# Attention and gated mixing on one core: the table that orders the program is replaced (2,239 pieces reordered, 219 on another engine)

## The chip, the cores and the metric

The kernel runs on one core of a Trainium2 chip. The core has five engines that run side by side, each through its own queue in order: TensorE (PE in the rows, its weight loads PEld), VectorE (DVE), ScalarE (ACT), GpSimd (POOL) and SyncE (SP), which here issues nearly all DMAs. Engines wait for each other by semaphores. The metric is the device time of one execution in microseconds; lower is better.

## The reference

```python
def _attn_ref(q, k, v):                      # q, k, v: 8 x 8 heads x 576 x 64
    k_p = k.reshape(B, H, Sp, pool, D).mean(axis=3)      # pool = 8, Sp = 72
    v_p = v.reshape(B, H, Sp, pool, D).mean(axis=3)
    scores = scale * np.matmul(q, k_p.transpose(0, 1, 3, 2))
    attn = np.exp(scores - max); attn = attn / (sum + 1e-09)
    return np.matmul(attn, v_p)

def _moe_ref(x, w_theta, w_tok_r, w_tok_i, w_ch):        # x: 8 x 576 x 512
    theta = x @ w_theta
    zr, zi = x * np.cos(theta), x * np.sin(theta)
    y = np.einsum('ts,bsd->btd', w_tok_r, zr) + np.einsum('ts,bsd->btd', w_tok_i, zi)
    u = x + y
    return u + np.maximum(u @ w_ch, 0.0)
```

The four weights arrive as 8-byte floats and are turned into 4-byte ones on the core.

## The kernel before, in words

The kernel is a set of generators, one for each small job. Each `yield` ends one piece: an instruction or a few that belong together. The string `SCHEDULE` names the pieces in the order in which they are written into the program; a word is the name of a generator, and a last letter v, g or a says whether VectorE, GpSimd or ScalarE does this piece where there is a choice. Since every engine goes through its queue in order, the table sets the order on all engines, and the order of SP's loads as well. No other code decides the order.

The jobs, with the batch as first number: `k`, `v` load keys and values, `K`, `V` pool them by 8; for batch 0 TensorE does the pooling (tiles `kpp`, `vpp`, L608, L610). The second half of `K` turns the pooled keys (`pk` L619 and `pkr` L629, both on TensorE) and copies them to the one tile `kpT`, which all score matmuls read. `Q` loads and turns queries (`pq` L670, tile `qT`). `S` makes scores (`s`, L762), their maximum, exponential and normalisation (`en`). `E` turns the attention of a batch by 16 small DMAs (L913), `X` multiplies with the values (`pv` L964). `T` (L991 to L1062) makes the angles (`pt`), sines and cosines and the product with x, which it writes to the tile `z`: for the last tokens of batch 0 the line of ScalarE is L995, of VectorE L997 and L1051, then the sine L1053 and the product L1055. `Z` splits a slice of `z` in a high and a low part (`zh`, `zl`), `M` mixes tokens with it (`py`, L1091, 27 matmuls a piece group), `F` is the last product with `w_ch` and the output (`pf`, L1119, L1135). `h`, `w`, `W` and `c` convert and turn the weights; `w_theta` arrives by way of `WTh_st` and becomes `ths`. `D` is a warm-up: 12 matmuls of the identity with itself, whose result nothing reads:

```python
    def warm_up():
        p = bank([P, 512], "av", "warm")
        for _ in range(12):
            nc.tensor.matmul(p[:, 0:P], ident, ident, start=True, stop=True)
        yield
```

The first `py` needs all of `z` of batch 0, so all nine token tiles of both weights and the whole of attention for batch 0 stand ahead of it. From there to the end each batch's `M` and `F` are woven with the next batches' `S`, `X` and `T`.

Of the kernel before, what the change touches and what calls it, by code (L numbers as in the profile page):

```python
# [1255 lines left out]
```

## Time and profile before

| | |
|---|---|
| median of 3 runs | 596.73 us (596.09 to 597.28) |
| the profiled execution | 598.02 us, span 596.2 us |
| PE busy | 580.1 us, 97% of the span |
| DVE, POOL, ACT busy | 456.2, 362.3, 319.0 us |
| DMA | 56.88 MB, mean 95 GB/s |

The profiled execution took 598.02 us on its own clock, 1.8 us more than the span between its first and last instruction, and 1.3 us more than the median of the runs.

### The profile page before, as it was taken

Reading aid. Unit: us, or ns where it says so; the run is one execution under the profiler, and the core shown is the slowest. Engines: PE = TensorE matmul, PEld = TensorE weight load, DVE = VectorE, ACT = ScalarE, POOL = GpSimd, SP = SyncE. Lnnn points to the kernel's source line nnn. Section 1 sums busy time; section 2 is a strip of 40 time slices with the busy share of each in tenths; the row PEclk is TensorE's granted clock in tenths of the full one; section 3 lists DMA queues with packets and bytes.
Section 4 is the critical chain, followed back from the end, with each engine's and each line's share of the span. In section 5 each row is a group of like instructions: output and inputs, shape, how many; then the busy total and the mean of one; then the engine's idle time right before and its main releaser. Section 6 shows DMA issues by size and latency. Waiting matters only on the chain.

```text
span 596.2 us, 11701 instructions
## 1 busy us (share of the span) xinstructions
PE 580.1 (97%) x4072; PEld 540.2 (91%) x4072; DVE 456.2 (77%) x857; ACT 319.0 (54%) x684; POOL 362.3 (61%) x517
## 2 busy tenths in 40 slices
PE   8799989999999999999999999999999999999996
PEld 7577879988999989999999999999999999999996
DVE  5989988888878897578969888887867688555434
ACT  3989987766457664186336663355434464432100
POOL 5562646567867885786878773754757665342620
PEclk9999979999999999999999999999999999999999
DMA  7995221576354273552555253562522310201214
GB/s 229 263 328 120 73 71 46 121 128 120 96 95 98 64 147 67 129 103 78 97 117 111 65 125 92 105 124 45 90 62 61 73 29 15 57 1 30 41 20 82
DMA packets 174203, 56.88 MB, mean 95 GB/s; under 512 B 148416, under 2 KB 162752, under 8 KB 174144
## 3 DMA queue, kind: packets, MB, share of 16 engines
q1 hardware_dynamic: 169280, 55.55, 42.1%
q10 hardware_dynamic: 4864, 0.59, 0.6%
q8 instruction: 32, 0.52, 0.4%
q14 instruction: 27, 0.22, 0.1%
HBM read 37.81 MB, written 9.44 MB: 79 GB/s over the span
## 4 chain that ended last, share of the span: by engine, by line
PE 81%; DVE 9%; ACT 5%; SPq 2%; issue 2%; DMA 1%; POOL 0%; DVEq 0%; POOLq 0%; ACTq 0%
PE py L1091 34%; PE pt L991 14%; PE pf L1119 14%; PE pv L964 6%; PE s L762 5%; PE px L1034 2%; SPq L913 1%; PE warm L310 1%; ACT e_eps L805 1%; PE kpp L608 1%; PE s L754 1%; PE vpp L608 1%; DVE mx L796 1%; DVE g L997 1%; SPq L642 1%
## 5 line engine op out<-in xcount | busy, mean ns | idle before, releaser
L1091 PE MATMUL py<-WTh,zh 128*128 128x256 f32 (+1 forms) x576 | 88.1, 298 | 0.7 <-DVE z L1060 0.6
L1091 PE MATMUL py<-WTl,zh 128*128 128x256 f32 (+1 forms) x576 | 87.3, 295 | 0.0
L1091 PE MATMUL py<-WTh,zl 128*128 128x256 f32 (+1 forms) x576 | 86.4, 296 | 0.0
L1091 PEld LDWEIGHTS py<-WTh,zh 128*128 128x128 f32 x576 | 80.4, 190 | 1.3 <-ACT zh L213 0.9
L1091 PEld LDWEIGHTS py<-WTl,zh 128*128 128x128 f32 x576 | 80.5, 189 | 0.2
L1091 PEld LDWEIGHTS py<-WTh,zl 128*128 128x128 f32 x576 | 78.6, 188 | 0.6
L198 POOL TENSOR_TENSOR zl<-z,zh 128x384 fp32r<-128x384 f32 (+1 forms) x80 | 63.8, 828 | 15.3 <-ACT zh L213 12.7
L198 POOL TENSOR_TENSOR en<-e_eps,ri 128x256 f32<-128x256 f32 (+3 forms) x66 | 38.3, 601 | 37.0 <-DVE ri L821 22.2
L995 ACT ACTIVATE g<-pt,c_magic 128x512 f32<-128x512 f32 x35 | 24.0, 686 | 54.7 <-PE pt L991 52.3
L1119 PE MATMUL pf<-uh,chh 128*128 128x256 f32 (+1 forms) x256 | 44.8, 298 | 0.5 <-DVE xb L1124 0.5
L1119 PE MATMUL pf<-uh,chl 128*128 128x256 f32 (+1 forms) x256 | 44.7, 296 | 0.0
L1119 PE MATMUL pf<-ul,chh 128*128 128x256 f32 (+1 forms) x256 | 44.0, 294 | 0.0
L991 PE MATMUL pt<-th,xh 128*128 128x512 f32 x148 | 41.8, 404 | 0.7 <-DVE xh L215 0.4
L991 PE MATMUL pt<-th,xl 128*128 128x512 f32 x148 | 40.5, 395 | 0.1
L991 PE MATMUL pt<-tl,xh 128*128 128x512 f32 x148 | 40.3, 394 | 0.0
L762 PE MATMUL s<-kpT,qT 128*128 128x144 f32 x256 | 38.4, 294 | 1.7 <-DVE ri L821 1.1
L1119 PEld LDWEIGHTS pf<-uh,chh 128*128 128x128 f32 x256 | 38.0, 188 | 2.3 <-DVE xb L1124 1.0
L1097 DVE TENSOR_TENSOR xb<-py,xb 128x320 f32<-128x320 f32 x32 | 15.2, 479 | 31.8 <-PE py L1091 31.8
L997 DVE SCALAR_TENSOR_TENSOR g<-g,pt 128x512 f32<-128x512 f32 x35 | 23.8, 681 | 18.9 <-ACT g L995 18.6
L762 PEld LDWEIGHTS s<-kpT,qT 128*128 128x128 f32 x256 | 34.9, 194 | 3.2 <-issue 1.4
L1119 PEld LDWEIGHTS pf<-uh,chl 128*128 128x128 f32 x256 | 37.4, 188 | 0.2
L1119 PEld LDWEIGHTS pf<-ul,chh 128*128 128x128 f32 x256 | 37.3, 188 | 0.0
(275 smaller groups left out, 1407.5 us busy)
## 6 DMA issues: line engine op xcount, KB each, us to landing
kpst<-in_k_dram SPq DMA_DIRECT2D x15, 512.0 KB, 4.3
vpst<-in_v_dram SPq DMA_DIRECT2D x28, 256.0 KB, 4.1
qsst<-in_q_dram SPq DMA_DIRECT2D x96, 72.0 KB, 3.2
eraw<-G SPq DMA_DIRECT2D x144, 40.0 KB, 1.9
out_dram<-R SPq DMA_DIRECT2D x112, 40.0 KB, 1.7
out_dram<-R SPq DMA_DIRECT2D x112, 32.0 KB, 1.7
eraw<-G SPq DMA_DIRECT2D x48, 60.0 KB, 2.0
WTh_st<-in_moe_w_theta_dram SPq DMA_DIRECT2D x4, 512.0 KB, 9.1
```

The costliest lines, as they stand in the source:

```text
L198: nc.gpsimd.tensor_tensor(out[:, r], a[:, r], b[:, r], op)
L310: nc.tensor.matmul(p[:, 0:P], ident, ident, start=True, stop=True)
L608: nc.tensor.matmul(main[:, 2 * j : 2 * j + 2, :], ident, st[:, :, D * r : D * r + D], **steps[r])
L762: nc.tensor.matmul(scs[c // 2][:n, 2 * SP * (c % 2) : 2 * SP * (c % 2 + 1)], qT[:, c, t0 : t0 + n], kpT[:, c, :], start=True, stop=True,)
L964: nc.tensor.matmul(pv[:, :gn], l, r, start=i == 0, stop=i == len(terms) - 1)
L991: nc.tensor.matmul(pt, l[:, c, :], r[:, c, :], start=i == 0, stop=i == 11)
L995: nc.scalar.activation(g, pt, AF.Identity, bias=c_magic)
L997: nc.vector.scalar_tensor_tensor(g, g, MAGIC, pt, ALU.subtract, ALU.subtract)
L1034: nc.tensor.transpose(px[:, P * c : P * c + P], x[:, c], ident)
L1091: nc.tensor.matmul(py[:, :n], l[:, kk, :], r[:, kw, t], start=i == 0, stop=i == 3 * NK - 1)
L1097: nc.vector.tensor_tensor(u, py[:, :n], u, ALU.add)
L1119: nc.tensor.matmul(pv[:, :n], l[:, kk, o], uhl[r][:, kk, t], start=i == 0, stop=i == 11)
```

## The change

Only `SCHEDULE` changes. The same 2,239 words stand in it in another order, on average 10.6 places away from where they stood, and 219 words end in another letter: 56 from VectorE to GpSimd and 44 back, 37 from VectorE to ScalarE and 33 back, 26 from GpSimd to ScalarE and 23 back. The instructions, tiles and buffers are the same.

```diff
 SCHEDULE = """
-k0.0 D K0.0 h0 h0 h0v h0v h0 h0 h0g k0.1 K0.0a K0.1 Q0.0 Q0.0 Q0.0v K0.1a K0 K0a h0 h0v h0 h2 h2 h2g h2v h2 k0.2 h1
-Q0.1 K0.2 K0.2a K0 K0a S0.0 S0.0 h1 h1a Q0.1 Q0.1v h1a h1 h1 h1g Q0.4 Q0.4 S0.0 S0.0 h2 Q0.4v S0.1 S0.1 S0.1 S0.1 k1.2
...
+k0.0 K0.0 K0.0a h0 h0 k0.1 K0.1 K0.1a K0 K0a h0g h0v h0 h0 h0v Q0.0 Q0.0 h0 k0.2 K0.2 K0.2v K0 K0v h0v Q0.0a S0.0 h2
+S0.0 h2 h2g h2a h2 h1 h1 Q0.1 Q0.1 D Q0.3 h0 Q0.1v S0.1 k1.2 h1v h1a S0.0 S0.0 h1 h1 S0.1 S0.1 S0.1 Q0.2 Q0.2 Q0.2v h2
...
```

Three places show what this does to the queues.

The first is TensorE's queue at the start of the program. Before:

```order
1 L310 MATMUL warm<-ident 128x128 x12
2 L608 MATMUL kpp_132<-kpst_0_117,ident 128x128 x8
3 L608 MATMUL kpp_132<-z,ident 128x128 x8
4 L670 MATMUL pq_0_166<-ident,qsst_0_164 128x128 x4
5 L619 MATMUL pk_173<-ident,kp_152 64x128 x4
6 L428 MATMUL ths_181<-WTh_st,ident 128x512
7 L429 MATMUL ths_181<-WTl_st,identr 128x512
8 L610 MATMUL kpp_132<-kprst_192,ident 64x64 x8
9 L629 MATMUL pkr_205<-ident,kpr_153 64x64
10 L762 MATMUL s_0_208<-kpT,qT_163 128x144 x4
11 L670 MATMUL pq_1_217<-ident,qsst_0_164 128x128 x4
12 L670 MATMUL pq_4_230<-ident,qst_228 128x64 x4
```

And in the changed kernel:

```order
1 L608 MATMUL kpp_119<-kpst_0_117,ident 128x128 x8
2 L608 MATMUL kpp_119<-z,ident 128x128 x8
3 L619 MATMUL pk_145<-ident,kp_128 64x128 x4
4 L670 MATMUL pq_0_162<-ident,qsst_0_160 128x128 x4
5 L428 MATMUL ths_167<-WTh_st,ident 128x512
6 L429 MATMUL ths_167<-WTl_st,identr 128x512
7 L610 MATMUL kpp_119<-kprst_170,ident 64x64 x8
8 L629 MATMUL pkr_181<-ident,kpr_129 64x64
9 L762 MATMUL s_0_186<-kpT,qT_159 128x144 x4
10 L670 MATMUL pq_1_202<-ident,qsst_0_160 128x128 x4
11 L310 MATMUL warm<-ident 128x128 x12
12 L762 MATMUL s_1_0_223<-kpT,qT_159 128x144 x2
```

The warm-up has moved from the first place to behind the first scores and the second block of queries (`pq_1`), and ahead of the second scores (`s_1`); the queries `pq_4` went further back.

The second place is SP's queue of loads at the start; `kprst` with 64x512 is the last part of a batch's keys, `z` stands in for buffers of queries and of values, `wraw` is a block of token weights. Before:

```order
8 L663 DMA qsst_0_164<-in_q_dram 128x8x64
9 L663 DMA qst_228<-in_q_dram 64x8x64
10 L564 DMA kprst_268<-in_k_dram 64x512
11 L663 DMA z<-in_q_dram 128x8x64 x2
12 L406 DMA WTh_st<-in_moe_w_theta_dram 128x1024
13 L457 DMA wraw_0_359<-in_moe_w_tok_r_dram 128x1152
14 L552 DMA kpst_1_390<-in_k_dram 128x2x512
15 L555 DMA z<-in_v_dram 64x2x512 x4
```

And in the changed kernel:

```order
7 L663 DMA qsst_0_160<-in_q_dram 128x8x64
8 L663 DMA z<-in_q_dram 128x8x64
9 L564 DMA kprst_229<-in_k_dram 64x512
10 L663 DMA z<-in_q_dram 128x8x64
11 L406 DMA WTh_st<-in_moe_w_theta_dram 128x1024
12 L663 DMA qst_315<-in_q_dram 64x8x64
13 L457 DMA wraw_0_372<-in_moe_w_tok_r_dram 128x1152
14 L555 DMA z<-in_v_dram 64x2x512 x4
15 L566 DMA vprst_418<-in_v_dram 64x1x512
16 L552 DMA kpst_1_444<-in_k_dram 128x2x512
```

One block of queries now stands ahead of `kprst` of batch 1, and the four loads of batch 0's values stand ahead of `kpst_1`, the 512 KB of batch 1's keys.

The third place is ScalarE's queue just before the first `py`, where the keys of batch 1 go into `kpT` and the last part of `z` is made. Before:

```order
96 L995 ACTIVATE g_4_923<-pt_4_889,c_magic 128x512
97 L213 CAST WTh<-wt_8_911 128x128
98 L1042 ACTIVATE xaspare<-xaspare,c_cos 128x512
99 L1053 ACTIVATE sn_4_935<-g_4_923,c_half 128x512
100 L213 COPY kpT<-pk_948 64x4x72
101 L213 COPY kpT<-pk_948 64x3x72
102 L213 COPY kpT<-pk_948 64x8
103 L213 COPY kpT<-pkr_956 64x64
104 L213 CAST zh_0_959<-z 128x2x9x64
```

And in the changed kernel:

```order
100 L995 ACTIVATE g_4_931<-pt_4_916,c_magic 128x512
101 L213 CAST WTh<-wt_8_945 128x128
102 L213 COPY kpT<-pk_954 64x4x72
103 L213 COPY kpT<-pk_954 64x3x72
104 L213 COPY kpT<-pk_954 64x8
105 L1042 ACTIVATE xaspare<-xaspare,c_cos 128x512
106 L1053 ACTIVATE sn_4_943<-g_4_931,c_half 128x512
107 L213 CAST zh_0_968<-z 128x2x9x64
108 L213 CAST zh_1_971<-z 128x2x9x64
```

The three copies from `pk` now stand ahead of the cosine (L1042) and the sine (L1053); the copy from `pkr` has left ScalarE and stands in VectorE's queue, behind the products L1047 and L1055 that end `z`. On TensorE the queries `pq_4` of batch 1, which stood between the scores `s` and the first `py`, now stand some 20 rows earlier.

## Rows read from the trace of the kernel before

**Rows 1.** The page: span, busy time of each engine, its share, instructions

```profile
span 596.2 us, 11701 instructions
PE 580.1 (97%) x4072; PEld 540.2 (91%) x4072; DVE 456.2 (77%) x857; ACT 319.0 (54%) x684; POOL 362.3 (61%) x517
```

**Rows 2.** Windows: length; PE, PEld, DVE, ACT, POOL busy; PE clock, DMA, GB/s

```profile
0.00:20.00 20.00, 16.83 (x116) 14.71 (x116) 13.57 (x27) 10.56 (x35) 9.21 (x18) 1.00 0.82 229
20.00:40.00 20.00, 17.37 (x121) 12.55 (x120) 16.95 (x35) 17.89 (x83) 14.12 (x22) 1.00 1.06 317
40.00:60.00 20.00, 19.84 (x117) 14.21 (x115) 19.55 (x39) 18.41 (x32) 5.39 (x8) 1.00 0.60 155
60.00:80.00 20.00, 17.10 (x106) 14.52 (x105) 17.75 (x33) 18.31 (x35) 14.04 (x18) 0.94 0.25 79
```

**Rows 3.** Waits of PE from 100 us to its end: us in total, times, longest

```profile
PE py L1091 <- DVE z L1060: 0.6, 1, 0.6
...
PE pt L991 <- DVE g L997: 0.2, 1, 0.2
```

**Rows 4.** Timeline of PE, 0 to 34 us: start, us, what, [idle before]

```profile
1.36 5.12 PE L310 MATMUL warm<-ident 128*128 128x128 f32 x24 [1.36 <-POOL ident masks.py:199]
6.54 2.05 PE L608 MATMUL kpp<-kpst,ident 128*128 128x128 f32 x16
8.95 2.05 PE L608 MATMUL kpp<-z,ident 128*128 128x128 f32 x16 [0.35 <-ACT kp L213]
...
14.51 1.25 PE L762 MATMUL s<-kpT,qT 128*128 128x144 f32 x8
...
17.20 1.25 PE L762 MATMUL s<-kpT,qT 128*128 128x144 f32 x8 [0.62 <-DVE qT L215]
...
21.11 1.22 PE L762 MATMUL s<-kpT,qT 128*128 128x144 f32 x8 [1.08 <-DVE ri L821]
...
28.39 3.83 PE L608 MATMUL vpp<-z,ident 128*128 128x128 f32 x32 [0.84 <-ACT wsrc_a L377]
```

**Rows 5.** The waits of PE's sequencer at L608 for the keys' loads

```profile
L608 PEldq EVENT_SEMAPHORE  x2: 51/51/51, 4.4 to 8.2; - x2
```

**Rows 6.** Timeline of SP's queue, 5 to 21 us

```profile
5.63 2.66 SPq L663 DMA_DIRECT2D qst<-in_q_dram  x1
14.07 0.49 SPq L564 DMA_DIRECT2D kprst<-in_k_dram  x1
...
18.26 2.81 SPq L555 DMA_DIRECT2D z<-in_v_dram  x4
```

**Rows 7.** Timeline of PE, ACT and DVE around the first py

```profile
72.93 1.08 PE L991 MATMUL pt<-th,xl 128*128 128x512 f32 x4
...
77.14 0.78 ACT L213 COPY kpT<-pk 64x288 f32<-64x288 f32 x3
77.60 0.67 DVE L1055 TENSOR_TENSOR z<-px,sn 128x512 f32<-128x512 f32 x1
...
77.97 0.31 PE L629 MATMUL pkr<-ident,kpr 64*64 64x64 f32 x1 [2.46 <-ACT kpT L213]
...
78.22 2.29 PE L762 MATMUL s<-kpT,qT 128*128 128x144 f32 x8
...
78.55 1.15 ACT L213 CAST zh<-z 128x1152 fp32r<-128x1152 f32 x1
...
80.44 0.69 PE L670 MATMUL pq<-ident,qst 64*128 64x64 f32 x4
...
81.05 2.29 PE L1091 MATMUL py<-WTh,zh 128*128 128x256 f32 x9
```

**Rows 8.** Windows, same columns as rows 2

```profile
78.00:81.00 3.00, 3.00 (x13) 2.54 (x13) 1.33 (x3) 1.93 (x3) 1.55 (x1) 0.50 0.03 8
81.00:84.00 3.00, 3.00 (x16) 2.95 (x15) 2.93 (x6) 2.64 (x6) 0.00 (x0) 0.50 0.00 0
...
85.00:86.00 1.00, 1.00 (x9) 1.00 (x8) 1.00 (x3) 1.00 (x8) 0.00 (x0) 1.00 0.53 74
```

More of the change, by code (lines that the diff above doesn't have):

```diff
@@ new lines @@
+T1.0g T1.0 M0.1.1a M0.3.1 S1.4v Q2.0 Q2.0 S1.4 S1.4a S1.4 S1.4 S1.4a k2.0 K2.0g T1.0 M0.3.0g M0.1.0a T1.0 T1.0 k2.2
+S1.4 X1.2.1 X1.2.1v K2 v2.0 F0.3.0 K2a X1.2.2 M0.0.0v X1.2.2a M0.3.0g F0.3.0 K2.2g K2 X1.2.0 T1.0 T1.0 M0.1.0g F0.3.0
+T1.0 X1.2.0v M0.0.1g V2.0v X1.2.3 X1.2.3a T1.2a T1.2g X1.2.3g M0.1.1g M0.3.1 T1.0a T1.0 T1.0 T1.0 Q2.1 Q2.1 T1.1a
+T1.1g M0.3.1 M0.3.1g T1.2 T1.2 T1.2 T1.2 v2.1 V2.1g V2g K2a Q3.0 T1.2 T1.2 T1.2 T1.2a T1.2 S2.0 S2.0 T1.1 T1.1 T1.1
+T1.2 T1.2 F0.3.0 T1.3g S2.1 T1.1 T1.1 T1.4v F0.2.0 T1.4v T1.1 T1.1 T1.1a T1.1 T1.1 F0.2.0 T1.1 F0.2.0 k3.0 F0.2.0
@@ new lines @@
+M1.0.1g S3.2 S3.3g S3.3v S3.4 T2.1 E2.2g E2.2v S3.4 S3.4 M1.2.1 M1.2.1 M1.2.1 T2.1 F0.0.1 S3.0 X2.2.3 X2.2.3a k4.2
+S3.3 X2.2.2 X2.2.2a S3.4v S3.4g X2.2.1 V3.1g X2.2.0 X2.2.0a S3.4 X2.2.1v T2.2a M1.3.0a M1.2.1 M1.2.1a M1.3.1 M1.3.1
+M1.3.1a T2.2v M1.3.1v M1.2.1v V3a V3v V3 V3g S3.0 T2.1 T2.1 V3g M1.2.0 S3.0 M1.2.0 M1.2.0 M1.2.0 T2.1 T2.1 T2.1
+M1.2.0v M1.2.0v T2.1a T2.1 F1.1.1 F1.1.1 T2.4a S3.0 K4.2g F1.3.1 F1.1.1 M1.0.0v E3.2 E3.2 S3.0g E3.2a F1.1.1 F1.1.1
+k4.0 S3.0g S3.1 S3.1 S3.1 F1.1.1 F1.3.1 F1.3.1 F1.3.1 F1.2.1 F1.3.1 F1.3.1 F1.2.1 T2.1 T2.1 F1.2.1 F1.2.1 v4.2 M1.3.0g
@@ new lines @@
+S5.2 S5.2 T4.0 T4.0 T4.0 S5.2g T4.0 T4.0 S5.3 S5.2v S5.3 S5.3 S5.3 T4.0 M3.1.0 M3.3.0 M3.3.0 M3.3.0 E4.2 E4.2 T4.0a
+V5.0g T4.1g T4.1 T4.1 T4.0 T4.0 M3.3.0 S5.2 T4.0 M3.3.0v S5.4 S5.3g S5.3v S5.4 F2.1.1 S5.3 E4.2a E4.2a E4.2v S5.4
+E4.2g S5.4 S5.4v S5.4g S5.4 M3.2.1 M3.2.1 M3.2.1 M3.2.0 v6.1 M3.2.0 M3.2.0 M3.0.0g X4.2.3 X4.2.3a X4.2.0 X4.2.0a
+X4.2.1 X4.2.2 V5g V5g V5 V5g X4.2.2a X4.2.1v T4.4a T4.2a M3.2.1 M3.2.1a M3.2.1g M3.1.0g S5.0 S5.0 T4.2v T4.1 T4.1
+T4.3a T4.1 S5.0 S5.0 S5.0g S5.0g Q6.0 T4.1 M3.3.1 T4.1 T4.1a T4.1 M3.3.1 M3.3.1 T4.2 T4.2 M3.3.0v T4.2 M3.3.1 M3.3.1v
@@ new lines @@
+M3.3.1g V6.1g T4.1 T4.1 T4.2 T4.2 F3.1.1 F2.3.1 F3.1.1 M3.2.0 F3.1.1 F3.1.1 F3.1.1 S5.1 E5.2 T4.3g E5.2 S5.1 M3.1.0g
+T4.2 T4.2 T4.2a T4.2 T4.2 V5g F3.3.1 k6.0 F3.3.1 F3.3.1 F3.3.1 S5.0 F3.1.1 E5.2a F3.3.1 F3.3.1 E5.2a E5.2g E5.2v
+F3.2.1 F3.2.1 F3.2.1 F3.2.1 F3.2.1 F3.2.1 F3.0.1 K6.0g F3.0.1 F3.0.1 S5.1 T4.3 T4.3 T4.2 F3.0.1 F3.0.1 T4.3 T4.3 S5.1
+X5.2.1 X5.2.1a X5.2.2 X5.2.2a X5.2.3 T4.3 X5.2.0 M3.2.0a F3.0.0 F3.0.0 X5.2.0v X5.2.3a S5.1g T4.4v T4.3 T4.3 S5.1v
+S5.1 T4.3a T4.4g k6.2 T4.3 K6.2g T4.4v T4.3 F3.0.1 T4.3 M3.2.0v T4.4 T4.4 T4.4 T4.4 T4.4 F3.0.0 F3.0.0 F3.0.0 k6.1
@@ L146 @@
+F7.3.1 F7.3.1 F7.3.1v M7.3.0 F7.2.1 F7.2.1 M7.3.0 M7.3.0g F7.2.1 M7.2.0 F7.2.1 F7.2.1 M7.2.0 M7.2.0 M7.2.0 F7.2.1v
+M7.2.0g M7.2.0g F7.0.1 F7.0.1 F7.0.1 F7.0.1 M7.3.0v F7.0.1 F7.0.1v F7.0.0 F7.0.0 F7.0.0 F7.0.0 F7.0.0 F7.0.0v F7.1.1
+F7.1.1 F7.1.1 F7.1.1 F7.1.0 F7.1.0 F7.1.0 F7.1.1 F7.1.1v F7.1.0 F7.1.0 F7.1.0v F7.3.0 F7.3.0 F7.3.0 F7.3.0 F7.3.0
+F7.3.0v F7.2.0 F7.2.0 F7.2.0 F7.2.0 F7.2.0 F7.2.0v
 """
```

202 lines of the change are left out of this document (89 added, 113 removed).

## The prediction

> **What bounds the kernel now.** I read the page first. TensorE is busy for 580.1 of 596.2 us [rows 1]; no other engine comes near. So a new order can win no more than what TensorE waits, what it does at half rate, and what it does for nothing. I looked for these three in that order.
>
> The waits come from the view of waits, asked for the stretch from 100 us on: the longest is 0.6 us, and all five entries of that answer (the first and the last stand in [rows 3]) add up to 1.9 us. After 100 us there is next to nothing to win, and a lot to lose. Before 100 us it is otherwise. The windows of 20 us [rows 2] show TensorE idle for 3.2, 2.6, 0.2 and 2.9 us in the first four, 8.9 us in all. There VectorE and ScalarE are the busy ones: 16.95 and 17.89, 19.55 and 18.41, 17.75 and 18.31 us of 20 between 20 and 80 us. The head is thus held by three things at once: loads up to 40 us (DMA share 0.82 and 1.06), VectorE and ScalarE after that, and the order in which TensorE stands in its queue.
>
> Half rate is read from equal rows. The same eight score instructions take 1.25 us at 14.51 [rows 4] and 2.29 us at 78.22 [rows 7], and the windows give a granted clock of 0.50 for 78 to 84 us and 1.00 for 85 to 86 [rows 8]: those are 1.2 and 2.4 GHz. What came before the fall was TensorE's longest wait, 2.46 us from 75.5 to 77.97 [rows 7]. The start is also at half rate: the warm-up's 24 instructions take 5.12 us, 0.213 each, while 16 pooling instructions of the same shape take 2.05 us behind it [rows 4], some 0.12 each. The window of 0 to 20 us prints 1.00 all the same, so for the start I go by the spacing, not by the clock column.
>
> **The change part by part.**
>
> *Warm-up away from the front.* TensorE's sequencer saw the first keys land at 4.4 and the second at 8.2 us [rows 5], but the warm-up held the engine until 6.5 [rows 4]. In the new queue the first pooling starts at 4.4, without a clock that has been raised: 16 times 0.213 is 3.4, so it ends at 7.8 instead of 8.6. The second pooling needs ScalarE's copy of the first (0.35 by the gap in rows 4) and the load of 8.2, and starts at 8.3 instead of 8.95. If it runs at half rate for its first half it takes (3.4 + 1.8) / 2 = 2.6 and ends at 10.9, which is when it ends before (8.95 + 2.05 = 11.0). I count 0. From below: full rate from 8.3, a gain of 0.7. From above: half rate to the end, 11.7, a loss of 0.7, and more if the half rate lasts (first rival).
>
> *Warm-up behind `pq_1`.* At full rate its 24 instructions cost 24 x 0.11 = 2.7 us (0.213 halved, which is what the pooling instructions show but for the last one's run-out). They lie where TensorE waited: `pq_1` ends at about 16.1 and the next scores begin at 17.20, of which 0.62 us are idle [rows 4] and 0.46 are `pq_4`, which is moved away. So the second scores begin at 16.1 + 2.7 = 18.8, 1.6 later. Behind them the third scores waited 1.08 us for VectorE [rows 4]; about half of the delay is taken up there, since VectorE does the same copies after the same matmuls. I take 1.1 of the 1.6 as what reaches the exponentials and through them `vpp` at 28.39. Bounds: 0 (all of it disappears in waits) and 1.6.
>
> *Loads.* SP issues in order, and in [rows 6] nothing leaves it between 5.63 + 2.66 = 8.3 and 14.07 us, when `kprst` of batch 1 may be overwritten: its buffer is free only when TensorE has pooled batch 0's rest. The new queue puts one block of queries ahead of that wait and takes the 512 KB of `kpst_1` from in front of the values. At the 317 GB/s of the second window [rows 2] 512 KB take 1.7 us, so the values land that much sooner. TensorE was idle for 0.84 us before `vpp` [rows 4]; more than this cannot be won there: 0.8. Who is later now is `kpst_1`; its pooling is GpSimd work of batch 1, and GpSimd is busy for 14.12 and 5.39 us of 20 in the windows from 20 and 40 us, so it is covered. If that cover failed, the price is again 1.7 us.
>
> *Load of VectorE and ScalarE before the first `py`.* Of the first 330 words, 12 go from VectorE to ScalarE, 11 back, 4 from VectorE to GpSimd, 3 back, 1 from GpSimd to ScalarE. With the mean of like instructions VectorE's work ahead of the first `py` falls by about 2.6 us and ScalarE's rises by about 3. The four windows have 67.8 for VectorE and 65.2 for ScalarE [rows 2]; after, the larger of the two is about the same. I take 0.5 us of gain for the wait chains that cross both, with 0 and 2.6 (VectorE's relief) as ends.
>
> *The keys of batch 1 and the end of `z`.* Before: the last `pt` frees TensorE's queue at about 73.9, `pk` is through at 75.5, ScalarE's copies to `kpT` come only at 77.14 to 77.92, since cosine and sine stand ahead of them, `pkr` goes at 77.97, the scores and `pq` fill 78.22 to 81.05, and `py` starts at 81.05, though `zh` was done at 79.7 [rows 7]. After: the three copies (0.78) run first, at about 75.35 to 76.15, so `pkr` goes at 76.2 and six of the eight score instructions are through by 77.1. The sine then ends 0.3 to 0.4 later; L1055 ends at about 78.5 (78.27 before), and the copy from `pkr` stands behind it on VectorE, so the last two score instructions wait until 78.8. `zh` (1.15) ends at about 79.8, and `py` can start there: 1.25 earlier than before. The `pq` that stood in between (0.69 at half rate, 0.4 at full) is now paid earlier: the gain is 0.8. The wait has not gone: instead of one of 2.46 there are three, of about 0.85, 1.7 and 0.75. I assume that the clock falls as before and costs what it did. Bounds: if none falls, what ran at half rate from 78.22 to 84 runs at full, that is 1.04 for the scores, 0.3 for `pq` and 1.5 for the 16 `py` of 81 to 84 us [rows 8], 2.8 more; if it falls later and more of `py` is hit, 1.5 less.
>
> *After 100 us.* Whatever the order, the matmuls are the same. Of the 1.9 us of waits the 0.6 before `py` of batch 4 is where the new queue leaves more TensorE work between the last `pt` and that `py`; I take 0.5. Bounds: 1.9 won; lost up to 2.6, one more wait as long as all idle time of the second window [rows 2].
>
> **Sum.** 0 + 1.1 - 0.8 - 0.5 - 0.8 - 0.5 = -1.5 us. On the profiled execution: 596.2 - 1.5 = 594.7 of span, plus the 1.8 around it 596.5; the runs' median is 1.3 below that execution, so **595.2 us**, 0.25% under 596.73. Runs of the same kernel differ by up to 0.2% from the fastest to the slowest, which is about what a measurement can tell from no change.
>
> **The rivals.**
>
> *The clock stays low until the warm-up (slower).* In the trace, pooling found a raised clock because 5.1 us of dense, waiting-free work stood ahead of it; at 78 to 81 us TensorE was busy all the time with scores and `pq` and the clock stayed at 0.50, and was back at 1.00 only behind the dense first `py` [rows 8]. The new start has real work with gaps: the copy after each pooling, the loads. If the clock is raised only in the warm-up, then all between 8.3 and `pq_1` takes double: TensorE's work there is 16.1 - 8.95 less 0.65 of waits, 6.5 us, so `pq_1` ends at 8.3 + 13 + 0.65 = 22, the warm-up runs mostly at half rate (5.1 at most) to 26 or so, and the second scores begin 8 to 9 us later than at 17.20. Loads and conversions go on meanwhile, but from 40 to 80 us VectorE and ScalarE have 0.45 and 1.6, then 2.25 and 1.7 us of slack [rows 2], so most is not caught up: 4 to 8, I take 5. Time 600. It decides if the spacing at 12 us is 0.2 rather than 0.11. The Trainium skill (TensorE: Matmul & The Clock Gate, Part 1: The HAM clock gate) calls the low rate the default and says that sustained activity releases it, which speaks against taking the warm-up from the front; the warm-up's spacing in rows 4 agrees. By that rule alone the first pooling is at half rate for certain, as in my sum; whether the second is, it leaves to how dense the work is.
>
> *The clock does not fall before the first `py` (faster still).* Three short waits in place of a long one: 2.8 us more, 592.4. For it: the single wait is broken up. Against: TensorE has work for under half of the 4.5 us.
>
> *The order wins nothing.* The first `py` hangs on `zh`, `zh` on the sine and L1055, and these move by -0.1 to +0.2 us; if `py` then waits where it did, gains and the warm-up's cost cancel: 596.7.
>
> **How the numbers follow.** Chances: the forecast 0.36 (its own range 594.0 to 596.4), clock low until the warm-up 0.28, no fall of the clock 0.18, nothing won 0.18. Faster by over 0.2% means under 595.5: 0.6 of the forecast and the second rival, 0.42 with a little from the others. Slower means over 597.9: the first rival and a few hundredths of unforeseen waits, 0.30. Same: 0.28. With 2 in 10 left out the range goes from 591.0 (no fall and the other terms at their ends) to 600.8 (the clock low, at a little over the price I took).
>
> **What would show it.** Right: pooling at 4.4, spacing 0.21 at first and 0.11 by 11 us; the warm-up's 24 instructions in about 2.7 us near 16 to 19; `vpp` at 28 to 29; waits of TensorE after 100 us under 3 us in all; `py` of batch 0 at about 79.5. Wrong: a warm-up of over 4 us (first rival), a first `py` after 83, or a wait of over 1 us after 100 us, most likely behind the small DMAs of `E`, whose place on SP I did not cost.

## The result

The changed kernel takes **600.64 us** (median of 15 executions, 598.27 to 603.27); the kernel before took 596.55 on the same chip (15 executions). The ratio is 1.0056 with an interval of 1.0037 to 1.0076: slower by 0.56%, some 3.3 us, where a gain of 1.5 was forecast. The time lies inside the range, the sign is wrong. The ratios are taken over all executions and are not quite the quotients of the medians.

One more number is used throughout. Each execution comes with its mean granted clock of TensorE. One less this mean, times the span, is the **lost clock** in us. In the 15 executions it is 6.3 us on the mean (the mean clock was 0.989 or less in ten of them); for the kernel before, on the chips of the experiments below, it is 2.3 to 3.1 us.

### The profile page after: what moved, and what is told of

The parts are those of the page before. It is cut to its first block, busy times and chain, and to the rows that moved or that the text cites. A ratio compares the mean times of both kernels' runs of the same rounds, so it can differ in the third digit from the quotient of the medians.

```text
span 597.7 us, 11703 instructions
## 1 busy us (share of the span) xinstructions
PE 580.0 (97%) x4072; PEld 540.2 (90%) x4072; DVE 445.8 (75%) x843; ACT 328.7 (55%) x690; POOL 364.1 (61%) x530
## 4 chain that ended last, share of the span: by engine, by line
PE 81%; ACT 5%; SPq 4%; DVE 2%; POOL 1%; issue 1%; DMA 1%; DVEq 0%; ACTq 0%; POOLq 0%
PE py L1091 36%; PE pf L1119 16%; PE pt L991 14%; PE pv L964 7%; PE s L762 4%; SPq L913 3%; PE px L1034 2%; ACT e_eps L805 1%; SPq L1135 1%; PE s L754 1%; POOL er L198 1%; DMA out_dram<-R 1%; PE wt L474 1%; ACT WTh L213 0%; PE pk L619 0%
## 5 line engine op out<-in xcount | busy, mean ns | idle before, releaser
L198 POOL TENSOR_TENSOR zl<-z,zh 128x384 fp32r<-128x384 f32 (+1 forms) x76 | 60.7, 831 | 27.9 <-ACT zh L213 22.5
L213 ACT CAST zh<-z 128x1152 fp32r<-128x1152 f32 x24 | 27.2, 1153 | 24.8 <-PE py L1091 18.5
L991 PE MATMUL pt<-th,xl 128*128 128x512 f32 x148 | 40.4, 395 | 0.0
L817 ACT ACTIVATE e_eps<-e_eps 128x576 f32<-128x576 f32 (+1 forms) x30 | 20.6, 687 | 30.4 <-DVE e_eps L813 30.0
```

Of the source, the lines that this page charges most:

```text
L198: nc.gpsimd.tensor_tensor(out[:, r], a[:, r], b[:, r], op)
L213: nc.scalar.copy(out, src)
L817: nc.scalar.activation(e[:n], e[:n], AF.Exp, scale=scale)
L991: nc.tensor.matmul(pt, l[:, c, :], r[:, c, :], start=i == 0, stop=i == 11)
```

## The profile after

The page, answering [rows 1]: TensorE's work is the same, VectorE lost 10 us and ScalarE gained 10.

```profile
span 597.7 us, 11703 instructions
...
PE 580.0 (97%) x4072; PEld 540.2 (90%) x4072; DVE 445.8 (75%) x843; ACT 328.7 (55%) x690; POOL 364.1 (61%) x530
```

This profiled execution (599.47 us, mean clock 0.991) is one of the better ones: it is only 1.5 us longer than the one of before. Its first windows, answering [rows 2], in the same columns:

```profile
0.00:20.00 20.00, 14.45 (x101) 12.94 (x102) 8.51 (x22) 10.26 (x31) 9.98 (x18) 1.00 0.84 234
20.00:40.00 20.00, 17.86 (x135) 13.37 (x133) 16.92 (x38) 18.69 (x88) 12.42 (x19) 1.00 1.03 299
40.00:60.00 20.00, 20.00 (x98) 13.38 (x97) 17.85 (x34) 16.62 (x29) 7.23 (x10) 0.91 0.55 144
60.00:80.00 20.00, 17.99 (x120) 15.21 (x118) 17.41 (x32) 18.42 (x36) 12.99 (x19) 1.00 0.35 94
```

The third row is the news: TensorE is busy all the time, does 98 instructions where it did 117, and its clock is 0.91 where it was 1.00. PE's timeline at the start, answering [rows 4]:

```profile
4.59 3.76 PE L608 MATMUL kpp<-kpst,ident 128*128 128x128 f32 x16 [4.59 <-POOL chh_st L347]
8.70 2.51 PE L608 MATMUL kpp<-z,ident 128*128 128x128 f32 x16 [0.35 <-ACT kp L213]
...
16.71 2.84 PE L310 MATMUL warm<-ident 128*128 128x128 f32 x24
19.39 1.15 PE L762 MATMUL s<-kpT,qT 128*128 128x144 f32 x8
...
28.63 3.84 PE L608 MATMUL vpp<-z,ident 128*128 128x128 f32 x32
```

The second pooling takes 2.51 us, between the 3.76 of half rate and the 2.05 of [rows 4]: the clock rose in the middle of it, long before the warm-up. The warm-up takes 2.84. `vpp` starts at 28.63 without a wait. Up to here nearly all is as forecast; only the first scores come 0.68 us later than in [rows 4], at 15.19. Then comes what was not forecast, in PE's timeline and in windows around it:

```profile
35.43 0.60 PE L964 MATMUL pv<-eh,Ve 128*128 128x256 f32 x2
35.95 0.69 PE L964 MATMUL pv<-er,Vr 32*128 32x256 f32 x2
37.17 0.70 PE L964 MATMUL pv<-eh,Ve 128*128 128x256 f32 x2 [0.52 <-DVE xa L970]
...
39.01 0.70 PE L964 MATMUL pv<-eh,Ve 128*128 128x256 f32 x2
...
40.26 1.97 PE L428 MATMUL ths<-WTh_st,ident 128*128 128x512 f32 x2
41.25 1.42 PE L429 MATMUL ths<-WTl_st,identr 128*128 128x512 f32 x1
42.46 0.41 PE L474 MATMUL wt<-ident,wsrc_a 128*128 128x128 f32 x1
...
43.80 0.29 PE L474 MATMUL wt<-ident,wsrc_a 128*128 128x128 f32 x1
...
43.99 0.30 PE L474 MATMUL wt<-ident,wsrc_a 128*128 128x128 f32 x1
```

```profile
36.00:40.40 4.40, 3.81 (x17) 1.92 (x17) 3.15 (x9) 4.30 (x22) 1.14 (x4) 1.00 1.04 313
40.40:43.80 3.40, 3.40 (x11) 2.17 (x12) 2.85 (x5) 1.11 (x2) 2.98 (x4) 0.50 0.96 339
...
81.40:84.00 2.60, 1.96 (x8) 1.26 (x7) 1.63 (x5) 1.33 (x3) 0.62 (x1) 0.50 0.00 0
84.00:88.10 4.10, 4.10 (x19) 4.10 (x20) 3.93 (x7) 4.07 (x12) 0.00 (x0) 0.50 0.02 4
88.20:90.00 1.80, 1.80 (x14) 1.80 (x14) 1.77 (x4) 1.77 (x12) 0.00 (x0) 1.00 0.26 80
```

From 40.4 to 43.8 us TensorE is at 1.2 GHz, a **second fall of the clock**. No long wait came before it: the longest idle time is 0.52 us, and TensorE was busy for 3.81 of the 4.40 us ahead. The fall at the first `py` is there too, later against the work than before [rows 8]. Around that `py`, answering [rows 7] (PE, then ScalarE and VectorE, each in its own order):

```profile
76.35 1.08 PE L991 MATMUL pt<-th,xl 128*128 128x512 f32 x4
...
80.17 0.24 PE L629 MATMUL pkr<-ident,kpr 64*64 64x64 f32 x1 [1.69 <-ACT kpT L213]
80.99 1.49 PE L762 MATMUL s<-kpT,qT 128*128 128x144 f32 x6 [0.58 <-DVE WTl L485]
83.03 0.85 PE L762 MATMUL s<-kpT,qT 128*128 128x144 f32 x2 [0.56 <-DVE kpT L215]
83.97 2.29 PE L1091 MATMUL py<-WTh,zh 128*128 128x256 f32 x9
...
79.32 0.80 ACT L213 COPY kpT<-pk 64x288 f32<-64x288 f32 x3
...
82.76 2.21 ACT L213 CAST zh<-z 128x1152 fp32r<-128x1152 f32 x2 [1.26 <-DVE z L1055]
...
82.06 0.67 DVE L1055 TENSOR_TENSOR z<-px,sn 128x512 f32<-128x512 f32 x1
```

The last four `pt` start 3.42 us later than in [rows 7], and the first `py` 2.92 later. The waits of PE after 100 us, answering [rows 3], are the whole answer of that view:

```profile
PE pv L964 <- POOL er L198: 1.2, 1, 1.2
PE pt L991 <- POOL xh L215: 0.6, 1, 0.6
PE pv L964 <- ACT xb L968: 0.5, 1, 0.5
```

That is 2.3 us where it was 1.9. Two of the forecast's signs of being wrong have come: a wait of over 1 us after 100 us (1.2), and a first `py` after 83 (83.97). The wait is not where the loss lies: from the first `py` to the end this execution takes 513.7 us, 1.4 less than the one before. The loss stands in the first 84 us, and the profile after has two candidates for it: the clock, and a chain that is longer of itself.

## The experiments

Pieces are counted from the front of `SCHEDULE`. The first `M0.0.0`, which issues the first `py`, is piece 352 in both tables, and the same 2,239 pieces stand on either side of any cut but for two to five. So a kernel can take the pieces up to a cut from one table and the rest, in its own order, from the other. The results first; "lost" is the mean lost clock of this kernel and of the kernel before on the same chip.

| run | what it is | median, before | ratio (interval) | lost, before |
|---|---|---|---|---|
| e1 | 1-351 changed, rest as before | 601.34, 596.80 | 1.0068 (1.0042-1.0093) | 6.2, 2.9 |
| e2 | 1-351 as before, rest changed | 593.98, 596.80 | 0.9951 (0.9925-0.9977) | 2.4, 2.9 |
| g4 | as e2, engines as before | 641.82, 596.45 | 1.0756 (1.0713-1.0798) | 10.8, 2.4 |
| e3 | changed, warm-up at the front | 601.14, 596.80 | 1.0065 (1.0041-1.0089) | 7.5, 2.9 |
| e4 | before, warm-up late | 596.90, 596.80 | 0.9986 (0.9964-1.0007) | 1.6, 2.9 |
| e7 | 1-182 changed, rest as before | 599.74, 596.60 | 1.0058 (1.0035-1.0081) | 5.0, 2.3 |
| h1 | 1-182 as before, rest changed | 596.79, 597.00 | 1.0000 (0.9976-1.0023) | 4.0, 3.1 |
| h2 | 113-182 as before, rest changed | 597.68, 597.00 | 0.9998 (0.9977-1.0019) | 3.3, 3.1 |
| h3 | 1-112 as before, rest changed | 597.35, 597.00 | 1.0000 (0.9979-1.0022) | 4.3, 3.1 |
| k1 | 1-325 as before, rest changed | 595.17, 596.69 | 0.9967 (0.9943-0.9991) | 1.9, 3.0 |
| k2 | 1-182, 326-351 as before, rest changed | 596.83, 596.69 | 1.0004 (0.9982-1.0027) | 3.7, 3.0 |
| g1 | changed, `ths` ahead of the second pair of `pv` | 599.00, 596.45 | 1.0048 (1.0029-1.0068) | 3.5, 2.4 |
| h4 | changed, `ths` one step later than in g1 | 598.45, 597.00 | 1.0017 (0.9997-1.0037) | 3.6, 3.1 |
| f1 | changed, filling behind `pk` | 599.56, 596.60 | 1.0042 (1.0027-1.0058) | 3.2, 2.3 |
| f2 | changed, filling at three places | 600.02, 596.60 | 1.0052 (1.0032-1.0072) | 0.7, 2.3 |
| g2 | g1 with half of f1's filling | 598.43, 596.45 | 1.0040 (1.0020-1.0060) | 1.8, 2.4 |
| f3 | e2 with filling behind `pk` | 594.45, 596.60 | 0.9973 (0.9955-0.9991) | 0.6, 2.3 |
| g3 | e2 with less filling | 593.59, 596.45 | 0.9949 (0.9925-0.9972) | 0.9, 2.4 |

### Head or tail: e1, e2, g4

The cut of e1, against the kernel before, and that of e2, against the changed one:

```diff
-... T0.4 T0.4 c0g c1 c0v K1 K1a K1 K1a Z0.0a c1 S1.0 S1.0 Q1.4 Z0.1g Z0.0v c1a M0.0.0 c1 c1 c1 Z0.1v ...
+... T0.4 T0.4 Z0.0a Z0.1a K1 K1v S1.0 S1.0 Z0.0v c1 c1a M0.0.0 c1 c1 c1 Z0.1v ...
```

```diff
-... T0.4 T0.4 Z0.0a Z0.1a K1 K1v S1.0 S1.0 Z0.0v M0.0.0 M0.0.0 M0.0.1 M0.0.1 c1 ...
+... c1 c0v K1 K1a K1 K1a Z0.0a c1 S1.0 S1.0 Q1.4 Z0.1g Z0.0v c1a v2.2 V1a M0.0.0 M0.0.0 M0.0.1 M0.0.1 c1 ...
```

> The first 351 pieces (everything up to the first py, about the first 84 us) in the order and on the engines of the changed kernel, the other 1,888 as before. Theory HEAD (the loss of 3 to 4 us arises before the first py: a second stretch at the 1.2 GHz level from 40.4 to 43.8 us, the later start, waits at 22 to 25 and at 37 us): 599.5 to 601, like the changed kernel. Theory TAIL (the loss arises behind the first py, in waits such as that of pv for er): 596 to 597, like the kernel before. If both share it: near 598.5.

> The reverse: the first 351 pieces as before, the rest in the order and on the engines of the changed kernel. Theory HEAD: 596 to 597. Theory TAIL: 599.5 to 601. The forecast's own term for the time after 100 us (a gain of 0.5, between a gain of 1.9 and a loss of 2.6) would be read here by itself: 594 to 599.

Both answers are clear. The head in the changed order costs 0.68%, 4 us; the rest in the changed order gains 0.49%, 2.9 us, more than the forecast's bound of 1.9 (which was for the time after 100 us, where this rest begins at the first `py`). The two do not simply add to the 0.56% of the whole, which is worse by some 2 us.

In g4 the order of e2's rest is kept, and each piece is done by the engine that did it before (184 letters, not 201):

```diff
-... S1.0 Z0.1v S1.0 S1.0g c1a c1v M0.0.1 M0.0.1 S1.0v V1g V1 ...
+... S1.0 Z0.1v S1.0 S1.0g c1v c1v M0.0.1 M0.0.1 S1.0g V1g V1 ...
```

> The head as before, the rest in the changed order but every piece on the engine that it had before: 201 or so of the moves of engine are taken back. If the gain of 2 to 3 us behind the first py comes from the order: 593.5 to 595. If it comes from the engines: 596 to 597. If order and engines only fit together: slower than 597.

45 us slower. The order by itself is no good order: here order and engines only fit together, and the gain of e2 can't be split between them.

### The warm-up's place: e3, e4

```diff
-k0.0 K0.0 K0.0a h0 ... Q0.1 Q0.1 D Q0.3 h0
+k0.0 D K0.0 K0.0a h0 ... Q0.1 Q0.1 Q0.3 h0
```

```diff
-k0.0 D K0.0 h0 ... Q0.2 Q0.2 h2v Q0.2v Q0.3 K1.2g Q0.3
+k0.0 K0.0 h0 ... Q0.2 Q0.2 h2v Q0.2v Q0.3 D K1.2g Q0.3
```

> The changed kernel with the one piece D (the twelve matmuls of the warm-up) back at the front, as the kernel before has it. Theory WARM-UP (its 2.8 us between pq_1 and the second s delay the chain of batch 0's first scores, and the granted clock comes late): a gain of 1 to 2 us on the changed kernel, 598.5 to 599.5. Theory CLOCK (the time hangs on the stretches at the 1.2 GHz level, whose second one at 40 us follows from the waits between 20 and 38 us, not from the start): the fall at 40 us stays, 600 to 601. If the fall at 40 us goes too: 596.5 to 597.5.

> The kernel before with D moved alone, from the front to between the two queries where the changed kernel has it (after pq_1, before the second s). Theory WARM-UP: 1 to 2 us slower than before, 597.5 to 598.5; with a new fall of the clock near 40 us: 599 to 600.5. Theory that the warm-up's place is worth nothing (start and cost cancel, as the forecast's two terms nearly did, -0.8 with +1.1): 596.5 to 597.

In e4 the piece came to stand a little later than its expectation says: ahead of `pq_3`, behind the second scores, at 20.27 us.

```profile
20.27 2.84 PE L310 MATMUL warm<-ident 128*128 128x128 f32 x24
...
35.63 0.59 PE L964 MATMUL pv<-eh,Ve 128*128 128x256 f32 x2
```

The first `pv` starts at 35.63, against 34.30 before: the chain is 1.3 us longer, where the start and the warm-up were costed at 0 and 1.1 together. Of the 1.3, 0.84 stand already at the first scores (15.35, against 14.51); but these start anywhere between 13.78 and 15.09 in the nine profiles with the old first 112 pieces, so how start and warm-up share it is not settled. The lost clock is 1.3 us shorter, and the time is the same. In e3 the warm-up's way back wins nothing either: its lost clock is the highest of all heads, 7.5. The warm-up's place by itself is not the cause.

### Which stretch of the head: e7, h1, h2, h3, k1, k2

Each is a cut like those above; for instance h1 against the changed kernel, and h2:

```diff
-k0.0 K0.0 K0.0a h0 ... Q1.0 Q1.0 v1.2 T0.0a T0.0v T0.0 w1.1 w1.1 w1.1a w1.1a k1.0 K1.0v
+k0.0 D K0.0 h0 ... T0.0a X0.2.3 X0.2.3v T0.0v v1.2 V1.2g X0.2.1 W0 Q1.0 Q1.0 T0.0 w1.1a w1.1a k1.0 K1.0v
```

```diff
-... S0.4 h1a h1 S0.4 S0.4 v0.1 V0.1 v0.2 V0.2 V0a V0 S0.2 S0.2a S0.3 k1.1 S0.3 S0.2 K1.1g X0.0.3 ...
+... S0.4 h1a h1 S0.4 S0.4 v0.1 k1.1 K1.1g V0.1 v0.2 V0.2 S0.3 V0a V0 X0.0.3 S0.3 w0.1 w0.1 ...
```

> Only the first 182 pieces (to the first softmax-weighted sums pv, about 46 us) as in the changed kernel, the rest as before. Lost clock below means one less the mean granted clock, times the span: on the mean of the runs 2.9 us before, 6.3 us in the changed kernel, 6.2 us with its whole head. Theory EARLY (the chain and the clock are both lost in the first 46 us): 600 to 601.5, lost clock 5 to 6.5 us. Theory KEYS (the clock is lost around the keys of batch 1 and the first py): 597.5 to 598.5 from the warm-up's place, lost clock near 3 us.

> The changed kernel with its first 182 pieces (about the first 46 us) as before. If the loss of the head lies in them, as the run with only these 182 changed said: 594 to 595.5, lost clock 2 to 3 us. If it lies between 46 us and the first py: 598 to 600.

> The changed kernel with pieces 113 to 182 (the last scores, the run of pv, the first token weights, 33 to 46 us) as before, and its own first 112 (loads, warm-up behind pq_1, up to vpp). Theory that the clock's fall near 40 us is the larger part: the fall goes, lost clock 2 to 3 us, 596.5 to 598 (the warm-up's place still costs its 1.3). Theory that the first 112 carry the loss: 599 to 600.5.

> The changed kernel with the first 112 pieces as before (warm-up at the front, loads as before), and its own run of pv behind them. Theory PV-RUN: the fall near 40 us stays, lost clock 5 to 7 us, 598 to 599.5. Theory that the first 112 carry it: 594.5 to 596, lost clock 2 to 3 us.

> The first 325 pieces as before, the rest as changed, so that the keys of batch 1, their copies to kpT and the queries pq_4 (pieces 326 to 351) stand as in the changed kernel. By the prediction's own term (0.8 gained there, or 2.8 more if the clock does not fall) 593 or less, against 594.0 with these pieces as before. If this place is where the 2.8 are lost: 596.5 to 597, lost clock 4 us.

> Pieces 183 to 325 (angles of batch 0, token weights, queries of batch 1, 46 to 75 us) as changed, the first 182 and pieces 326 to 351 as before, the rest as changed. If the 2.8 are lost in these: 596.5 to 597. If they are lost around the keys: 594.

The first 182 pieces, 46 us, carry the loss: alone they cost 0.58% (e7), and with them as before the changed kernel is level (h1). But neither half of them carries it. With 113 to 182 as before, or with 1 to 112 as before, the kernel is level just the same. It takes the changed start and the changed run of `pv` together. h2 came out as its first theory has it: 597.68, no fall of the clock near 40 us in its profile, 3.3 us lost. h3 came out as neither of its own has it: its profile does show the fall, `ths` at half rate from 38.31, and the kernel is level all the same.

Level is not e2's gain, though. Pieces 183 to 351 as changed take back 2.9 us (h1 against e2). Of them the place around the keys of batch 1 gives 0.9967 by itself (k1), the angles and weights ahead of it 1.0004 (k2). k2's 596.83 is the first case of its expectation, the loss in the angles and weights, and its interval is clear of e2's; k1's 595.17 lies between the cases of its own, and its interval overlaps both e2's and h1's. So the angles and weights cost something, and whether the keys do is not settled. In k1 the place that the forecast worked out can be seen alone, on PE:

```profile
76.74 0.24 PE L629 MATMUL pkr<-ident,kpr 64*64 64x64 f32 x1 [0.89 <-ACT kpT L213]
76.91 1.00 PE L762 MATMUL s<-kpT,qT 128*128 128x144 f32 x6
79.07 0.85 PE L762 MATMUL s<-kpT,qT 128*128 128x144 f32 x2 [1.16 <-DVE kpT L215]
80.00 2.29 PE L1091 MATMUL py<-WTh,zh 128*128 128x256 f32 x9
82.09 2.12 PE L1091 MATMUL py<-WTl,zh 128*128 128x256 f32 x9
84.01 2.19 PE L1091 MATMUL py<-WTh,zl 128*128 128x320 f32 x9
```

The first wait is 0.89 (forecast 0.85) and `py` starts at 80.00 (forecast 79.8), 1.05 us earlier than before. The order does there what it was read to do. But most of the 27 `py` shown are now at half rate, where it was 16: they take 6.05 us to the start of the next group, against 5.07 before, and the gain is gone.

### The clock: g1, h4, and the fillings

The kernel before has two `ths` of channel block 3, three rows of 128x512 on PE (the expectation of g1 says four), among its `pv`; the changed one has them behind the third pair, at 40.26. g1 and h4 move this one step back in between; both edits start from the first line:

```diff
-w0.1 S0.2v w0.1 w0.1v w0.1v X0.0.2 X0.0.2v w0.1 ... X0.0.0 X0.0.0v w0.1v w1.0a h3 h3a W0
+w0.1 S0.2v w0.1 w0.1v w0.1v h3 X0.0.2 X0.0.2v w0.1 ... X0.0.0 X0.0.0v w0.1v w1.0a h3a W0
```

```diff
+w0.1 S0.2v w0.1 w0.1v w0.1v X0.0.2 h3 X0.0.2v w0.1 ... X0.0.0 X0.0.0v w0.1v w1.0a h3a W0
```

> The changed kernel with one step of TensorE moved: the two ths of channel block 3 (four PE rows, 1.7 us at the full clock), which it has at 40.26 us behind the first three pv, go ahead of the pv that waits 0.52 us at 37.17; the kernel before has them at 37.29, between its second and third pv. Theory PV-RUN (the fall at 40.4 us follows from a run of short and narrow work with waits, 33.5 to 40.3 us, that nothing wide breaks): the fall goes in most executions, lost clock from 6.3 to 3 or 4 us, time 1.5 to 3 us below the changed kernel's, 597.5 to 599. Theory that the fall comes from earlier: lost clock near 6, time 600 to 600.5 (less the 0.5 wait).

> The changed kernel with the two ths of channel block 3 directly behind the second work of pv (37.2 us) and not ahead of it, where their bank is free and nothing waits. If the fall of the clock goes as it did with them ahead, and no wait comes in: lost clock 3 to 4 us, 598 to 598.8. If the fall comes back: 600 to 601.

In h4, the same places on PE and in the window that was at half rate:

```profile
36.87 0.70 PE L964 MATMUL pv<-eh,Ve 128*128 128x256 f32 x2 [0.52 <-DVE xa L970]
...
38.12 1.13 PE L428 MATMUL ths<-WTh_st,ident 128*128 128x512 f32 x2
38.68 0.80 PE L429 MATMUL ths<-WTl_st,identr 128*128 128x512 f32 x1
```

```profile
40.40:43.80 3.40, 3.26 (x25) 2.65 (x25) 2.55 (x5) 3.23 (x6) 1.46 (x4) 1.00 0.74 285
```

The wait of 0.52 is still there, the fall is not, and 25 instructions fit where 11 did. The last four `pt` start at 74.87, 1.5 us sooner than in the changed kernel (of which 0.3 stand already at `vpp`, 28.33), with the same waits of TensorE from 34 to 77 us:

```profile
PE pv L964 <- DVE xa L970: 0.5, 1, 0.5
PE pq L670 <- DVE g L997: 0.5, 1, 0.5
PE per L862 <- DVE Vr L687: 0.2, 1, 0.2
```

The mean clock was 0.993 or more in each of 12 executions of g1 and of h4; the changed kernel had 0.993 or more in two of 15. One step of TensorE, moved by 2 us, takes the loss from 0.56% to 0.17% (on two chips, each against the kernel before; the intervals just touch). In g1, with the same lost clock as h4, the ratio is 1.0048, hardly better than the changed kernel's. There the move waited 0.90 us for its bank, which still held scores that ScalarE was reading, where h4 has the 0.52; that covers some 0.4 of the 1.8 us between the two ratios, and the rest is not explained.

The profiles of all runs say more than these two. The clock was at half rate somewhere between 38 and 46 us in five of the six profiles whose run of `pv` is the changed one with nothing moved or filled into it (the changed kernel, e3, e7, f1 and h3; not e1), and in none of the 14 others. What it costs can be read between e1 and f1, whose first 337 pieces are the same:

```profile
75.06 1.08 PE L991 MATMUL pt<-th,xl 128*128 128x512 f32 x4
```

```profile
38.60 1.21 PE L969 MATMUL pv<-eh,Ve 128*128 128x256 f32 x2
...
77.50 1.08 PE L996 MATMUL pt<-th,xl 128*128 128x512 f32 x4
```

The first fence is e1's. In f1 `pv` takes 1.21 where it takes 0.70 at full rate, and the low clock lasts to about 45.5. From the start of `vpp` to these last four `pt` it is 46.06 us in e1 and 46.54 in h4, both without the fall, 47.72 in the changed kernel, 49.30 in f1, and 44.5 to 45.2 in the six profiles with the old order up to there. So where it comes the fall costs 1.2 to 3.2 us, and the chain without it is 0.9 to 2.0 longer than in the old order.

The other way is to fill TensorE's idle time with work that nobody reads: the generator of `D` gets further pieces, placed where TensorE waits.

```diff
             nc.tensor.matmul(p[:, 0:P], ident, ident, start=True, stop=True)
         yield
+        for i, n in enumerate((14,)):
+            p = bank([P, 512], "mm", f"fill{i}", bufs=2)
+            for _ in range(n):
+                nc.tensor.matmul(p[:, 0:P], ident, ident, start=True, stop=True)
+            yield
```

```diff
-K1 K1a W2 T0.3 T0.3
+K1 D K1a W2 T0.3 T0.3
```

> The changed kernel with 14 extra matmuls (ident by ident, 128 columns, result unused) behind the transposes pk of batch 1's keys, where TensorE waits 1.7 us for the copies of kpT. Theory CLOCK-BY-IDLE (the fall at the first py follows from this wait): lost clock drops by about 3 us, to 3 or 4, and the time by 2.5 to 3.5 us, to 597 to 598. Theory that the fall there does not depend on the wait: time as the changed kernel's or up to 0.5 longer, lost clock near 6.3.

> As the one with 14 extra matmuls, and 8 and 6 more ahead of the third and the fourth-to-last work of the first pv's (ahead of the pv that waits 0.52 us at 37.2 us, and of the next but one), which cost about 1 us of TensorE's time themselves. Theory CLOCK-BY-IDLE: the fall at 40 us goes too, lost clock under 2 us, time 595 to 597. Theory that the fall at 40 us follows from what lies before 35 us: lost clock as in the first of these two, time 0.5 to 1 us longer than it.

> As the one with the ths moved, and 7 extra matmuls (1.6 us by the 3.29 us that 14 took) behind pk of batch 1's keys, in the wait of 1.7 us. If the two falls of the clock are what made the head slower: lost clock under 2 us, time 595.5 to 597, level with the kernel before. If the extra chain of the head (1 us or more) counts as much: 597 to 598.5.

> The head as before with the rest as changed (594.0 in the earlier run), with 16 extra matmuls behind pk of batch 1's keys, where TensorE waits 2.5 us. Theory CLOCK-BY-IDLE: lost clock falls from 2.4 us to under 1, time 592 to 593. Theory that it does not depend on the wait: 594 to 594.5.

> The head as before with the rest as changed, and 10 extra matmuls (2.3 us) behind pk of batch 1's keys, inside the wait of 2.5 us, where 16 of them took 3.7 and delayed pkr by 1.2. Theory that the fall of the clock there costs what it costs at half rate: 592 to 593 (594 without them), lost clock near 1. Theory that it is covered by other waits: 594.

In f2 the two further pieces stand ahead of `X0.0.2` and `X0.0.0`, the second and third pair of `pv`, which its expectation calls by other numbers; the first of them waited 0.90 us for its bank, as in g1. g2 has 7, f3 16 and g3 10 in place of 14.

The clock does what it should: the lost clock falls from 6.3 to 3.2 with one filling and to 0.7 with three. The time hardly follows. The filling was sized wrongly by me, since each of these source matmuls shows as two rows of PE (14 as 28), so that 14 of them took twice the wait of 1.69 that they were to fill. In f1:

```profile
79.46 3.29 PE L315 MATMUL fill<-ident 128*128 128x128 f32 x28
82.68 0.24 PE L634 MATMUL pkr<-ident,kpr 64*64 64x64 f32 x1
```

So in f2 nearly all of the clock is back and the kernel is 0.52% slower all the same: filling costs TensorE's time, and TensorE has none to give. Where it was sized to the wait (g2, g3) the lost clock is low and the time is that of the same kernel without it, within the interval. The best versions are e2 and g3, half a per cent faster than the kernel before; between these two the runs don't decide.

## Why the prediction was wrong

**The start (0, bounds -0.7 and +0.7): inside its bounds.** Pooling at 4.59, the clock up in the second pooling, in spite of the gap of 0.35 ahead of it; the first scores 0.68 later. The first rival had the right time, 600, for a reason that did not occur: its sign was a spacing of 0.2 at 12 us and a warm-up of over 4 us, and the warm-up took 2.84. That 600.64 lies inside the range at all is luck, since this rival set the upper end of 600.8. The scatter was taken too small as well: 0.2% came from three runs, and the 15 executions of the kernel before run from 595.60 to 600.88, 0.9%.

**The warm-up behind `pq_1` (+1.1): about right in the chain.** The second scores begin 2.2 us later, 1.5 of it arising behind the first scores (forecast 1.6), and e4 shows 1.3 at the first `pv`, start and warm-up together. That e4 gets it back in clock was not in the sum.

**The loads (-0.8): not shown.** In this profile `vpp` has lost its wait of 0.84 and starts at 28.63, 0.24 after [rows 4], where +1.1 and -0.8 give +0.3. But e1's profile, with the same first 351 pieces, waits 1.01 us at `vpp` for the load of the values, and h3's, with the old loads, does not wait and starts at 27.05. In the nine profiles with the first 112 pieces as before `vpp` starts between 26.76 and 29.01, in the nine with them changed between 27.84 and 29.85, so one profile can't weigh a term of 0.8.

**VectorE and ScalarE before the first `py` (-0.5): wrong.** Without the fall at 40 us (h4's profile) the last four `pt` start at 74.87, 1.94 later than in [rows 7]. At the first `pv` h4 is 0.83 behind, mostly because four `pe` of the tokens that come next stand ahead of it (33.47 to 33.96 in the changed kernel); the other 1.1 arise from there to the last `pt`. TensorE is idle for 1.15 us in that stretch, above all in the two waits of 0.5, for `xa` and for `g`, against 0.61 before; and it is busy for 0.57 longer, since `pq_4` and a `px` now stand ahead of the last `pt` (the forecast counted `pq_4` with the keys). At the first `py` h4 is 1.43 behind. Counting an engine's work over 80 us said nothing of such waits.

**The keys of batch 1 (-0.8): the order right, the sum wrong.** k1 shows it. The copies were put at 75.35, a little ahead of the 75.5 at which by the same working `pk` is through; k1 has them 0.64 behind the start of `pk`. In the changed kernel they come at 79.32, since the last `pt` is 3.4 us late. And the step read "I assume that the clock falls as before and costs what it did". It falls when `py` is next, and not when scores and `pq` are, so more of `py` is hit: 6.05 us for the first 27 in k1 and 5.42 in the changed kernel, against 5.07 before, 0.4 to 1.0 of its bound of +1.5.

**The step that failed** is one that the sum does not have. It let the clock fall at the start and at the first `py` alone, because in the one profile of the kernel before it fell nowhere else. The changed kernel falls at 40.4 us too: by the rows, `ths` and the four pairs of `wt` behind it take from 40.26 to 43.80, 3.54 us; in h4 the step behind `ths` follows after 1.29, and four pairs of `wt` at the 0.19 that one takes from 43.80 on make 0.8, 2.1 together. So the fall cost 1.4 us in this execution, near the 1.2 between `vpp` and the last `pt`; in f1's profile it is 3.2 (against e1). In other executions more is lost, 6.3 us of clock on the mean against 3.6 in h4. In h4, without the fall, 0.56% becomes 0.17%; in g1, without it too, only 0.48%. An estimate by another way: in the 145 executions of the kernel before on five chips 1 us more of lost clock goes with 0.5 to 0.9 us more of time (a straight line through each chip's executions), so the 3.2 to 4.0 us of clock that the changed kernel loses more would make 1.6 to 3.6 us, where it is 3.3 slower. The fall is thus shown, and it costs time; that it is the larger part, ahead of the longer chain, is likely but not shown.

**After 100 us (-0.5, bounds -1.9 and +2.6): not by the way forecast.** The wait of 0.6 before `py` [rows 3] is gone from the list, but a longer one has come in its place, and the waits are 2.3 in all against 1.9. e2 gives 2.9 for all behind the first `py`. In its profile the time from the first `pf` to the last is within 0.2 us of before, and the gain lies mostly between the first `py` and there, part of it clock, since in e2's profile the clock did not fall there at all (the second rival's case); how the 2.9 splits is not settled.

Left open: why the changed start and the changed run of `pv` cost nothing one at a time and 0.56% together. A fall at 38.5 us is in h3's profile too, and h3's lost clock is 4.3 on the mean, so one half seems to make it possible and the other regular; that is argued, not shown.

## What to carry to other kernels

When a new order makes the same work slower, read the granted clock along the span before looking for waits: a stretch at half rate shows as a fully busy engine. Here it helped to put something wide in the middle of a run of narrow and short work, and to move it there from elsewhere: a step that had to be done anyway cost no wait of its own where its bank was free (h4) and 0.90 us where it was not (g1), while a filling costs what it takes. And cut a large reordering at a few places and run the halves: here a gain of half a per cent was hidden behind a loss of the same size, and keeping the old head kept it.

## What was not expected of the hardware

The clock fell with TensorE busy for 3.81 of 4.40 us and no idle time over 0.52, in a run of `pv` of which every second uses 32 rows. It stayed up when two `ths` of 128 rows by 512 columns stood among them, with the same wait of 0.52. It also stayed up in e1's profile, with nothing moved and that same wait, so the order makes the fall possible and does not bring it every time. What about the two `ths` decides was not separated. The Trainium skill (TensorE: Matmul & The Clock Gate, A second HAM failure mode: psum-queue depth-cycling) tells of a kernel that idled only briefly between groups of matmuls and whose clock oscillated. This trace is like it in the brief idle times, 0.59 us in all of the 4.40, but it shows one fall there and no oscillation.

The other way round, a long wait need not bring a fall. In e2 `pkr` waits exactly as long as in [rows 7], and the clock stays up through the first `py`:

```profile
78.61 0.24 PE L629 MATMUL pkr<-ident,kpr 64*64 64x64 f32 x1 [2.46 <-ACT kpT L213]
78.78 1.25 PE L762 MATMUL s<-kpT,qT 128*128 128x144 f32 x8
79.96 0.46 PE L670 MATMUL pq<-ident,qst 64*128 64x64 f32 x4
80.34 1.29 PE L1091 MATMUL py<-WTh,zh 128*128 128x256 f32 x9
```

The same nine `py` take 1.29 us here and 2.29 in [rows 7]. And the old head too can lose its clock elsewhere: g4's granted clock is 0.67 from 20 to 24 us, and in k2 the first 32 `vpp` take 5.44 us where [rows 4] has 3.83. So one profile does not tell how much a kernel loses of its clock; the mean clock of a dozen executions does, though not where.
